# Tiles of an attention and feed-forward kernel moved to multiples of 128 bytes in SBUF

## Chip, cores and metric

One core of a Trainium2 chip. The metric is the device time of one execution in microseconds (us), as a median of several runs. TensorE's granted clock is given by the profile as a share of 2.4 GHz.

## What is computed

Attention over 4 batches, 8 heads, 768 positions and 64 columns a head, with a window of 96 local and 8 global keys and a bias by distance, then a feed-forward layer 512 - 2048 - 512 with ELU, all in float32:

```python
scores = scale * np.matmul(q, k.transpose(0, 1, 3, 2))
bias = -slopes[:, None, None] * dist[None, :, :]
scores = np.where(keep, scores + bias[None, :, :, :], -1000000000.0)
a = np.exp(scores - np.max(scores, axis=-1, keepdims=True))
a = a / (np.sum(a, axis=-1, keepdims=True) + 1e-09)
x = np.matmul(a, v)             # (B, H, S, D) -> (B * S, H * D)
h = x @ w_in
g = np.where(h > 0.0, h, np.exp(np.minimum(h, 0.0)) - 1.0)
out = g @ w_out
```

## The kernel before

The 3072 rows are worked in 12 groups of 256 (two tiles of 128 positions each). For each group the attention of four pairs of heads is computed, and its result is kept in a tile `xh` as a high part (float32r, the type that TensorE takes in one pass) and a low part. The feed-forward layer then runs over 16 chunks of 128 hidden columns: three matmuls make one product in full precision (high x high, low x high, high x low).

There are two stages. In the first (groups 0 to 2, up to about 200 us) the weights are loaded and split into high and low parts on VectorE and ScalarE, and the plain products run: up at L780 (`three`, h<-xh,w), down at L738 (o<-w,gh, 512 columns). In the second (groups 3 to 11) the chunks are taken in pairs, and the down product is a scheme with seven block products in place of eight. Up is again L780 (h<-xh,w0s): the stationary operand is a block of 128 columns of the up weights, which come back from DRAM into a ring of four slots as `w0s`, the moving one is 256 columns of `xh`. Down is L840 (a<-w,gg, a<-ta,gg, a<-tb,gg): here the activations `gg` are stationary and 256 columns of the prepared down weights move. A group has 192 matmuls of L780 and 168 of L840; L780 runs 48 in a row for a pair of chunk pairs (24 in group 11), L840 runs 21 in a row for a chunk pair. Between the two, `z` is worked on by ScalarE (L708, L709) and VectorE (L710), and the attention of a later group is slipped in: its scores (L542; in the first stage L666, in plain float32), transposes (L562, L683) and the products with the values (L585, L700). A few matmuls at L1010 and L1019 fill gaps at the beginning; their results aren't used.

The order on every engine is found in advance by a planner (`Plan.order`) from due times and costs, and then written out as it is. A tile takes one of the named slots of its class (`SLOTS`); a slot is a tag in one of two pools, `w` for the weights (tags that begin with w) and `m` for the rest, laid behind the constants of pool `c`. Tiles are made by `sb` (L306) through `make` when their first writer is written out. `xh` has three slots: in the second stage the odd groups (3, 5, 7, 9, 11) lie in xh0 and the even ones (4, 6, 8, 10) in xh1. A tile begins at a multiple of 32 bytes within a partition, behind the tile before it.

Of the kernel before, what the change touches and what calls it, by code (L numbers as in the profile page):

```python
# [16 lines left out]
P = 128  # L17
# [3 lines left out]
WN = A0 + P  # L21
# [238 lines left out]
def act(n, psum=False, extra=0.0):  # L260
    return (("ACT", (55 if psum else 97) + 0.834 * n + extra, False),)
# [14 lines left out]
class Kernel:  # L276
# [29 lines left out]

    def sb(self, cls, name, shape, dtype=F32, slots=None):
        nm = self.n(name)
        return self.plan.tile(cls, nm, lambda s: (self.w if s[0] == "w" else self.m).tile(shape, dtype, tag=s, name=nm), slots)

    def bank(self, cls, name, shape, slots=None):
        nm = self.n(name)
# [20 lines left out]

    def consts(self):
        self.ident = self.const("ident", [P, P])
        self.tab0, self.tab1 = self.const("tab0", [P, P]), self.const("tab1", [P, WN])

        self.scale = self.const("scale", [P, self.NP])
        self.nmax = self.const("nmax", [P, self.B * self.H * self.S // P])
# [274 lines left out]
    def softmax(self, b, h, t, st_, s, pr, st, i, d):  # L614

        nc, p = self.nc, self.plan
        lo = 0 if t else A0
        n = WN - lo
        at = (b * self.H + h) * (self.S // P) + t
        nm = self.nmax.t[:, at:at + 1]  # L620
        tab = self.tab1.t if t else self.tab0.t
        p.add((("DVE", 158 + 1.042 * n, False),), lambda e: nc.vector.tensor_tensor_reduce(  # L622
            pr.t[:, lo:], st_()[:, lo:], tab, -(2.0 ** -(h + 1)), 3.0e38, ALU.add, ALU.min, nm), [s], [pr], d - 4500)
        p.add(act(n, extra=200), lambda e: nc.scalar.activation(  # L624
            pr.t[:, lo:], pr.t[:, lo:], AF.Exp, bias=nm, scale=-1.0, accum_out=st.t[:, 0, i:i + 1]), [pr], [pr, st], d - 4000)
# [241 lines left out]
    def build(self):  # L867
# [24 lines left out]
        for n, (b, gi) in enumerate(groups):  # L892
# [6 lines left out]
            for hp in range(self.NP):  # L899
# [5 lines left out]
                if n > self.GS:  # L905
                    ahead = start[self.GS] + self.PERIOD * (4 * (n - self.GS - 1) + hp - 2) + self.VISIT
                    d, st = ahead + self.AFTER, 600.0
                todo.append((d if X_.get("rows") else last + 1, lambda b=b, gi=gi, hp=hp, n=n, d=d, st=st, X_=X_, ahead=ahead: self.pair(
                    b, gi, hp, *X[n], d, ahead, st, X_)))
                last = d  # L910
        todo.append((last + 1, lambda: self.visit(lambda: None, 0.0, [], [], last - self.AFTER + self.PERIOD)))
        for fc, d in wdue.items():
# [30 lines left out]

    PERIOD, SECOND, DOWN, DOWN2, VISIT, VALUES = 13200.0, 2890.0, 6730.0, 9250.0, 9245.0, 6720.0
    AFTER = 2 * PERIOD - VISIT + VALUES
    PASSES, SINCE = 2, 195000.0
    GS, KEEP, COMBO = 3, 100000.0, 0.0
    LATE, ASKED = 11, (2, 3, 4)
# [293 lines left out]
```

## Time and profile before

| | us |
|---|---|
| median of three runs | 678.94 (678.84 to 679.95) |
| the profiled execution, whole | 678.11 |
| its span in the trace | 676.3 |
| TensorE busy (share of the span) | 660.5 (98%) |
| weight loads, beside the matmuls | 611.2 (90%) |
| VectorE busy | 516.9 (76%) |
| ScalarE busy | 476.7 (70%) |

Matmuls are pipelined: one of 256 columns is shown with some 280 ns from its start to its end, but the next one starts some 115 ns later. So the time of a run of matmuls is read from the run, not from one of them.

### The profile page before, as it was taken

What the parts mean: (1) busy time and instruction counts of PE and PEld (TensorE: products, weight loads), DVE (VectorE), ACT (ScalarE), POOL (GpSimd) and SP (SyncE); (2) the same over time, 40 slices, a digit from 0 to 9 for tenths busy, and PEclk for the clock granted to TensorE, in tenths of its full rate; (3) what the DMA queues carried; (4) which work ended last, traced back from release to release, by engine and by line L of the source; (5) the groups of instructions that cost most, each with busy time, mean ns of one, the idle gap of its engine ahead of it and who ended that gap; (6) DMA issues with size and microseconds to landing.
All of it is one profiled execution on the core that took longest, in us unless ns stands there. A gap on an engine that the chain in (4) does not pass through costs nothing.

```text
span 676.3 us, 15974 instructions
## 1 busy us (share of the span) xinstructions
PE 660.5 (98%) x5950; PEld 611.2 (90%) x5950; DVE 516.9 (76%) x1515; ACT 476.7 (70%) x1254; POOL 39.4 (6%) x65
## 2 busy tenths in 40 slices
PE   8999999999999999999999999999999999999995
PEld 6677888888888999999999999999999999999995
DVE  7999999999997677667767866866776777765653
ACT  7998888757786667766767766676777767664542
POOL 3143002011210000000000000000000000000000
PEclk9999999999999999999999999999999999999998
DMA  7837978510257665766676657656766765663841
GB/s 265 311 95 259 377 280 322 214 43 19 57 162 244 218 226 170 235 207 228 202 223 232 204 194 223 251 161 211 251 209 203 242 224 163 212 232 135 253 153 37
DMA packets 52233, 137.75 MB, mean 204 GB/s; under 512 B 5682, under 2 KB 18738, under 8 KB 52146
## 3 DMA queue, kind: packets, MB, share of 16 engines
q1 hardware_dynamic: 51856, 136.24, 59.7%
q8 instruction: 49, 0.80, 0.5%
q10 hardware_dynamic: 290, 0.39, 0.2%
q14 instruction: 38, 0.31, 0.1%
HBM read 119.84 MB, written 16.78 MB: 202 GB/s over the span
## 4 chain that ended last, share of the span: by engine, by line
PE 81%; DVE 11%; ACT 3%; DMA 2%; issue 1%; POOL 0%; DVEq 0%; POOLq 0%; SPq 0%
PE h L780 34%; PE a L840 28%; PE o L738 5%; PE pv L585 4%; PE s L542 3%; PE t L562 3%; DVE g L450 2%; DMA rqv<-in_qkv_dram 2%; PE s L666 2%; PE pv L700 1%; DVE gl L331 1%; PE t L683 1%; DVE e L710 1%; ACT pr L624 1%; DVE g L426 1%
## 5 line engine op out<-in xcount | busy, mean ns | idle before, releaser
L780 PE MATMUL h<-xh,w0s 128*128 128x256 f32 x1728 | 210.9, 282 | 0.0
L780 PEld LDWEIGHTS h<-xh,w0s 128*128 128x128 f32 x1728 | 207.3, 190 | 0.1
L840 PE MATMUL a<-w,gg 128*128 128x256 f32 x864 | 140.9, 278 | 0.0
L323 ACT CAST gg<-z 128x384 fp32r<-128x384 f32 (+1 forms) x144 | 81.4, 566 | 73.3 <-PE a L840 35.3
L710 DVE SCALAR_TENSOR_TENSOR z<-z,h 128x512 f32<-128x512 f32 x72 | 49.5, 688 | 106.3 <-ACT z L709 101.9
L840 PEld LDWEIGHTS a<-w,gg 128*128 128x128 f32 x864 | 119.5, 188 | 0.0
L624 ACT ACTIVATE pr<-pr,nmax 128x232 f32<-128x232 f32 (+1 forms) x192 | 90.7, 473 | 6.3 <-DVE nmax L622 6.2
L780 PEld LDWEIGHTS h<-xh,w 128*128 128x128 f32 x576 | 81.6, 189 | 8.8 <-issue 1.4
L331 DVE TENSOR_TENSOR gg<-z,gg 128x512 fp32r<-128x512 f32 (+1 forms) x144 | 84.5, 619 | 5.4 <-ACT gg L323 5.1
L780 PE MATMUL h<-xh,w 128*128 128x256 f32 x576 | 87.4, 284 | 0.1
L708 ACT ACTIVATE z<-h 128x512 f32<-128x512 f32 x72 | 43.0, 597 | 49.0 <-PE h L780 48.3
L811 DVE TENSOR_TENSOR z<-z 128x128 f32<-128x128 f32 (+1 forms) x216 | 72.3, 335 | 5.4
L622 DVE CUSTOM_DVE_ANT_0 pr<-s,tab 128x232 f32<-128x232 f32 (+1 forms) x192 | 62.8, 376 | 15.0 <-PE s L542 14.7
L840 PE MATMUL a<-ta,gg 128*128 128x256 f32 x432 | 72.1, 278 | 0.0
L738 PE MATMUL o<-w,gh 128*128 128x512 f32 x192 | 59.4, 402 | 1.6 <-DVE ob L765 1.2
L840 PEld LDWEIGHTS a<-ta,gg 128*128 128x128 f32 x432 | 59.7, 188 | 0.0
L840 PE MATMUL a<-tb,gg 128*128 128x256 f32 x216 | 53.5, 309 | 0.0
L709 ACT ACTIVATE z<-z 128x512 f32<-128x512 f32 x72 | 45.4, 631 | 2.1
L840 PEld LDWEIGHTS a<-tb,gg 128*128 128x128 f32 x216 | 34.5, 188 | 8.9 <-issue 5.3
L738 PEld LDWEIGHTS o<-w,gh 128*128 128x128 f32 x192 | 32.1, 189 | 6.6 <-ACT pr L624 1.6
L624 ACT ACTIVATION_READ_ACCUMULATOR pr<-pr,nmax 128x1 f32 x192 | 37.1, 193 | 0.0
L608 ACT ACTIVATE pr<-pr,st 128x232 f32<-128x232 f32 (+1 forms) x66 | 29.3, 468 | 10.4 <-DVE st L644 9.1
(122 smaller groups left out, 932.3 us busy)
## 6 DMA issues: line engine op xcount, KB each, us to landing
w0s<-kept SPq DMA_DIRECT2D x144, 512.0 KB, 5.1
rk<-in_qkv_dram SPq DMA_DIRECT2D x45, 184.0 KB, 2.5
bits<-in_w_in_dram SPq DMA_DIRECT2D x16, 512.0 KB, 7.3
bits<-in_w_out_dram SPq DMA_DIRECT2D x16, 512.0 KB, 9.5
kept<-w SPq DMA_DIRECT2D x16, 512.0 KB, 4.3
rv<-in_qkv_dram SPq DMA_DIRECT2D x32, 256.0 KB, 5.0
rqv<-in_qkv_dram SPq DMA_DIRECT2D x13, 384.0 KB, 3.7
rqv<-in_qkv_dram SPq DMA_DIRECT2D x34, 128.0 KB, 3.0
```

The costliest lines, as they stand in the source:

```text
L323: self.nc.scalar.copy(out, x)
L331: self.on(e).tensor_tensor(out, x, y, ALU.subtract)
L608: self.nc.scalar.activation(out, x, AF.Copy, scale=sc)
L622: p.add((("DVE", 158 + 1.042 * n, False),), lambda e: nc.vector.tensor_tensor_reduce(pr.t[:, lo:], st_()[:, lo:], tab, -(2.0 ** -(h + 1)), ...
L624: p.add(act(n, extra=200), lambda e: nc.scalar.activation(pr.t[:, lo:], pr.t[:, lo:], AF.Exp, bias=nm, scale=-1.0, accum_out=st.t[:, 0, i: ...
L708: p.add(act(n, True), lambda e: nc.scalar.activation(out(), hx(), AF.Relu, scale=-1.0), [h], [ex], due)
L709: p.add(act(n), lambda e: nc.scalar.activation(out(), out(), AF.Exp, scale=-1.0), [ex], [ex], due)
L710: p.add(dve(n), lambda e: nc.vector.scalar_tensor_tensor(out(), out(), -1.0, hx(), ALU.add, ALU.max), [h, ex], [ex], due)
L738: nc.tensor.matmul(acc[i].t, g.t[:, i * P:(i + 1) * P], w2.t[:, s], start=fc == f0 and n == 0 and s == HI, stop=fc == f1 - 1 and n == 1)
L780: self.nc.tensor.matmul(hx(), w1.t[:, s, cc * P:(cc + 1) * P], xh.t[:, x, cc], start=n == 0 and cc == 0, stop=n == 2 and cc == self.NCC - 1)
L811: tt = lambda e, out, x, y, op: self.on(e).tensor_tensor(out, x, y, op)
L840: nc.tensor.matmul(acc[i].t[:, j], gg.t[:, x, g], w(s), start=c == x == s == 0 and n in (0, 2, 4, 6), stop=c == N7 - 1 and x == LO and n i ...
```

## The change

The constant `tab1` gets 8 more columns (32 bytes), of which the softmax reads what it read before. `sb` rounds the size of each tile up to a multiple of 128 bytes (`LINE` is 32 elements of four bytes) and gives the kernel the view of the shape that it asked for. A list of names, `ODD`, that would begin 64 bytes later is empty. Instructions, their order on each engine, their waits and the slots are the same as before; the addresses in SBUF differ. Where the built programs place the tiles, as bytes past a multiple of 128:

| tile | before | after |
|---|---|---|
| all slots of the weights (w0, w1, w0s, ta, tb, bits) | 96 | 0 |
| xh0, xh1, xh2 | 96, 32, 96 | 0 |
| gg; gh and gl | 32 | 0 |
| z in its slots z0, vd0, xh2 | 96, 32, 96 | 0 |
| qs, ks, rv, part | 32 | 0 |
| rqv, rk of the first stage | 96 (two of them 32) | 0 |
| pr in the second stage | 32 and 64 | 0 |
| tab0, tab1, ident | 0 | 0 |

`pr` grows from 928 to 1024 bytes, `rk` from 1472 to 1536, `st` from 48 to 128; the rest were multiples of 128 already, and change by where they begin.

```diff
     def sb(self, cls, name, shape, dtype=F32, slots=None):
         nm = self.n(name)
-        return self.plan.tile(cls, nm, lambda s: (self.w if s[0] == "w" else self.m).tile(shape, dtype, tag=s, name=nm), slots)
+        n = 1
+        for x in shape[1:]:
+            n *= x
+        first = self.LINE // 2 if name in self.ODD else 0
+
+        def make(s):
+            t = (self.w if s[0] == "w" else self.m).tile([P, -(-(first + n) // self.LINE) * self.LINE], dtype, tag=s, name=nm)[:, first:first + n]
+            if len(shape) > 2:
+                names = "abcd"[:len(shape) - 1]
+                t = t.rearrange(f"p ({' '.join(names)}) -> p {' '.join(names)}", **dict(zip(names, shape[1:])))
+            return t
+
+        return self.plan.tile(cls, nm, make, slots)
...
-        self.tab0, self.tab1 = self.const("tab0", [P, P]), self.const("tab1", [P, WN])
+        self.tab0, self.tab1 = self.const("tab0", [P, P]), self.const("tab1", [P, WN + self.LINE // 4])
...
-        tab = self.tab1.t if t else self.tab0.t
+        tab = self.tab1.t[:, :WN] if t else self.tab0.t
...
     AFTER = 2 * PERIOD - VISIT + VALUES
+    LINE, ODD = 32, ()
```

## Rows read from the trace of the kernel before

**Rows 1.** The page: span, busy time and share of TensorE, its clock in 40 slices.

```profile
span 676.3 us, 15974 instructions
...
PE 660.5 (98%) x5950; PEld 611.2 (90%) x5950; DVE 516.9 (76%) x1515; ACT 476.7 (70%) x1254; POOL 39.4 (6%) x65
...
PEclk9999999999999999999999999999999999999998
```

**Rows 2.** Stretches from:to us: length, busy us (and instructions) per engine, clock, DMA.

```profile
75.00:200.00 125.00, 123.45 (x850) 107.38 (x851) 124.00 (x316) 94.68 (x256) 14.57 (x18) 1.00 0.48 175
200.00:660.00 460.00, 458.90 (x4499) 440.60 (x4498) 317.70 (x936) 313.44 (x793) 1.62 (x3) 1.00 0.64 210
```

**Rows 3.** The page's chain of work that ended last, by engine and by line.

```profile
PE 81%; DVE 11%; ACT 3%; DMA 2%; issue 1%; POOL 0%; DVEq 0%; POOLq 0%; SPq 0%
PE h L780 34%; PE a L840 28%; PE o L738 5%; PE pv L585 4%; PE s L542 3%; PE t L562 3%; DVE g L450 2%; DMA rqv<-in_qkv_dram 2%; PE s L666 2%; PE pv L700 1%; DVE gl L331 1%; PE t L683 1%; DVE e L710 1%; ACT pr L624 1%; DVE g L426 1%
```

**Rows 4.** That chain in order of time: start us, length us, engine, tile, line, count.

```profile
494.32 5.45 PE h L780 x48
...
519.79 5.75 PE h L780 x48
533.14 5.75 PE h L780 x48
...
539.92 2.67 PE a L840 x21
543.90 2.58 PE a L840 x21
...
586.43 5.65 PE h L780 x48
...
632.05 2.88 PE h L780 x24
```

**Rows 5.** Timeline of TensorE: start us, length us, then what; even and odd group.

```profile
481.44 5.61 PE L780 MATMUL h<-xh,w0s 128*128 128x256 f32 x48
...
531.28 0.62 PE L840 MATMUL a<-ta,gg 128*128 128x256 f32 x4
...
532.98 5.92 PE L780 MATMUL h<-xh,w0s 128*128 128x256 f32 x48
...
540.66 0.63 PE L840 MATMUL a<-ta,gg 128*128 128x256 f32 x4
```

**Rows 6.** Timeline of weight loads at the filler matmuls; line L1019, mean of one below.

```profile
31.26 1.30 PEld L1019 LDWEIGHTS o<-w 128*128 128x128 f32 x11 [0.17 <-issue]
...
L1019 PEld LDWEIGHTS o<-w x11: 187/192/193, 31.3 to 32.4; 128*128 128x128 f32 x11
```

**Rows 7.** Chain up to 215 us: shares by line, then pieces in order of time.

```profile
by line: PE o L738 15.5%; PE h L780 15.2%; DVE g L450 6.4%; DMA rqv<-in_qkv_dram 5.2%; PE s L666 5.0%; PE pv L700 4.0%; DVE gl L331 3.8%; issue 3.5%; PE t L683 3.4%; DVE e L710 3.2%; ACT pr L624 2.9%; DVE g L426 2.5%; DVE w L331 2.3%; DVE g
...
12.28 4.15 DMA rqv<-in_qkv_dram
...
19.06 3.35 DMA rqv<-in_qkv_dram
...
34.69 0.98 PE s L666 x8
36.49 0.94 PE h L780 x8
...
38.45 0.98 PE s L666 x8
40.10 1.39 PE o L738 x6
```

**Rows 8.** Line views of L710 and L709 on z: ns min/median/max, first and last start.

```profile
L709 ACT ACTIVATE z<-z x72: 620/632/635, 206.1 to 662.2; 128x512 f32<-128x512 f32 x72
L710 DVE SCALAR_TENSOR_TENSOR z<-z,h x72: 670/689/690, 206.7 to 662.9; 128x512 f32<-128x512 f32 x72
```

**Rows 9.** DMA issues: count, size, median us to landing.

```profile
w0s<-kept SPq DMA_DIRECT2D x144, 512.0 KB, 5.1
```

## Prediction

> **What bounds the kernel now.** I read the page's first two parts, then the busy times by stretch, then the chain of work that ended last, first by line and then in order of time. TensorE is busy 660.5 of 676.3 us at a granted clock of 1.00, that is 2.4 GHz, and only the last slice shows less [rows 1]. From 200 to 660 us it stands still for about 1 us of 460, while VectorE is busy 317.7 and ScalarE 313.4 us; from 75 to 200 us VectorE is as full as TensorE, 124.0 of 125 us [rows 2]. The chain says the same: 81% TensorE, and two lines hold 62% of the span, the up products of L780 (34%) and the down products of L840 (28%) [rows 3]. So in the long second stage the spacing of these matmuls is the time. There are 1728 of L780 and 1512 of L840 in it, all 128x128 weights against 256 columns.
>
> The rows that matter are those of the same work at different speeds. In order of time, a run of 48 matmuls of L780 takes 5.75, 5.65 or 5.45 us, and a run of 21 of L840 takes 2.67 or 2.58 us [rows 4]. Per matmul 5.75 is 119.8 ns, 5.65 is 117.7, 5.45 is 113.5. The timeline gives the same with the pipeline's end in it: 5.92 against 5.61 us for 48, 0.63 against 0.62 for 4 of L840 [rows 5]. The clock is full in all of them and nothing is waited for, so only the operands differ. Instruction, shape and weight slots are the same in all groups of query blocks; what alternates is the slot of xh, the moving operand. Odd groups (3, 5, 7, 9, 11) read xh0, which starts 96 bytes past a multiple of 128, the offset of the weights; even groups (4, 6, 8, 10) read xh1, at 32. Each of the 17 runs of 48 and 6 of 24 on xh0 is of the slow kind (16 of them are in the list of long pieces). Of the 16 on xh1, 11 are 5.65 and 5 are 5.45. L840 has its moving weights at 96 and its stationary gg at 32, also different, and never the slow kind: counted from the starts of its matmuls, 40 of 72 runs are at 117.7 ns, 32 at 113.4.
>
> **What I take from that.** The start addresses of the two operands that TensorE reads at the same time (the columns of this matmul and the weights of the next) set the spacing. At 2.4 GHz 113.4 ns is 272 columns and 119.9 ns is 288: 17 and 18 times 16 columns of four bytes, so a step of 64 bytes. My reading, an estimate from these rows, is that operands are fetched in aligned pieces of 64 or 128 bytes, that 1024 bytes beginning 32 bytes off need a piece more, and that two streams that cross their borders together collide for another. Starting on a border takes the extra piece away.
>
> The Trainium skill, "SBUF — State Buffer", section "Who interferes with whom", says otherwise: TensorE never waits on anyone, and its two read ports are independent. By that the change is worth nothing and the sum is 678.1. The 5.75 and 5.45 us of equal work disagree [rows 4].
>
> **The change, part by part.**
> L780 on xh0: all operands now at 0. If each run goes at the fast spacing that the trace has, 17 x (5.75 - 5.45) + 6 x (2.88 - 2.72) = 5.1 + 0.9 = 6.0 us. L780 on xh1: 11 x (5.65 - 5.45) = 2.2 us. L840: 40 x (2.67 - 2.58) = 3.6 us. Together 11.8 us, all on the path: TensorE has no idle time there that it could fall into, VectorE and ScalarE have a third of the stretch free, and the weights of the ring land 5.1 us after their issue while a period of two chunks is 13.3 us (the distance of two 5.75 rows) [rows 2, 4, 9]. What is late next is still TensorE.
>
> How fast an aligned pair is, no row shows. From below, the weight load bounds it: the eleven filler matmuls of L1019 stream only 128 columns and their weight loads still come (1.30 - 0.19) / 10 = 111 ns apart [rows 6]. At 111 ns the gain is 17 x 0.42 + 6 x 0.22 + 11 x 0.32 + 5 x 0.12 + 21 x (40 x 0.0067 + 32 x 0.0024) = 8.5 + 4.1 + 7.2 = 19.8 us. From above it is 119.8 ns for all (the rival below). I take 113.4, a spacing that is there already and needs only that the worse two go. The Trainium skill, "TensorE: Matmul & The Clock Gate", section "Back-to-back issue gap", gives 262 cycles for 256 columns, which is 109 ns, and would make it some 26 us; the weight load of 111 ns speaks against so much.
>
> The first 200 us: in the chain up to 215 us L780 and L738 have 15.2 and 15.5% [rows 7], 32.7 and 33.3 us, of which 5.8 us belong to the first run of the second stage. So some 226 matmuls at about 118 ns (0.94 for 8) and 144 with 512 columns at 232 (1.39 for 6) [rows 7]. At 4.6 ns less each that is 1.0 + 0.7 = 1.7 us, but VectorE is full there and takes over; I count half, 0.8 us. The bounds are 0 and 3.5 (226 x 4.6 ns and 144 x (232 - 213), where 213 ns is 512 columns at 2.4 GHz).
>
> The other matmuls (L542, L562, L585, L666, L683, L700): half arrays or plain float32, some of them on operands at 0 or 64 already. L666 takes 0.98 us for 8 wherever it stands, though its keys begin at 96 in one half of the eight and at 0 in the other [rows 7]; I put these at 0, within 0.5 us either way. VectorE and ScalarE: z lies at 96 in one slot and at 32 in another, and 72 instructions of L710 take 670 to 690 ns, of L709 620 to 635 [rows 8]. They don't see these offsets; 0. DMA: the queues' bytes and order stay. On the chain they stand in three pieces of 3.4 to 4.2 us at the start [rows 7]; a tenth of that either way is 1 us, I take 0. Tiles grow by at most 96 bytes, and no slot, wait or instruction moves.
>
> **Sum:** 678.11 us of the profiled execution - 11.8 - 0.8 = 665.5. That execution is 0.83 us under the median of the three (678.94), so I expect a median of about 666.3 us, 1.9% less.
>
> **The rivals.**
> Equal offsets collide, on a border or off it. The slow kind is the one where both operands have the same offset, and now all have. For it: without exception, 17 runs of 48 and 6 of 24. Against: the fillers of L1019 read both operands from one tile at 96 and are 111 ns apart, so that equal offsets alone don't cost 7 ns; and the extra piece that gives two streams an uneven first step is gone. It decides if the pair at 0 and 0 behaves as the pair at 96 and 96: then L780 on xh1 loses 11 x 0.10 + 5 x 0.30 = 2.6 us and L840 21 x (40 x 2.1 + 32 x 6.4) ns = 6.1 us, while xh0 gains nothing: 8.7 us, 687.6 us.
> The middle spacing stays. The same operands of L840 run now at 113.4 and now at 117.7 for a whole run, which looks like two ways in which the streams can fall into step, and aligned ones may have both. With all at 117.7 xh0 gains 17 x 0.10 + 6 x 0.05 = 2.0, xh1 loses 1.0 and L840 32 x 0.09 = 2.9: 1.9 us slower, 680.8. With half of the runs so, about 5 us gained, 674.
> Nothing happens. If xh0 and xh1 differ for another reason than their offset to 128 (the slot's place in the memory, what writes nearby), or by the page's rule above, padding changes nothing: 678.9. Against it speaks that L840, in its own slots, keeps to the two faster kinds.
>
> **How the numbers follow.** Forecast 0.56, the middle spacing 0.16, equal offsets collide 0.20, nothing 0.08. The range goes from 678.9 - 19.8 - 3.5 = 655.6 (weight load as the bound, all of the early gain) to 681.0 (all at the middle spacing) and leaves out the collision. A measurement of this kernel tells about 0.2% (1.4 us) from no change. Faster: 0.56 + 0.13 of the middle spacing = 0.69. Same: 0.06 of nothing and 0.03 of the middle = 0.09. Slower: 0.20 + 0.02 = 0.22.
>
> **What would show it.** In the chain of the changed kernel, the runs of 48 should be 5.45 us or a little less in odd and even groups alike, and those of 21 2.58 or less. Rows of 5.75 everywhere, L840 at 2.7 and above, mean the collision; a mix of 5.65 and 5.45 the middle. If odd groups are still slower than even ones, the offset to 128 was not the reason. The forecast is wrong, too, if matmuls get faster and the span doesn't: then VectorE's waits for ScalarE's z or TensorE's idle time must have grown.

## The result: 1.1% slower, and what the profile after shows

| | before | after |
|---|---|---|
| median, us (4 runs each) | 678.89 (677.8 to 679.95) | 686.5 (684.7 to 687.12) |
| ratio, 95% interval | | 1.0111 (1.0096 to 1.0125) |
| the profiled execution, its span | 678.11, 676.3 | 684.7, 682.9 |
| TensorE busy, us | 660.5 | 668.0 |

The forecast of 666.3 us was wrong in size and in sign: the range went to 681.0, and the time lies above it. What came true is the rival "equal offsets collide", priced at 687.6.

The page of the kernel after answers [rows 1] and [rows 3] (line numbers are now 12 higher: L780 is L792, L840 is L852, L738 is L750).

```profile
span 682.9 us, 15974 instructions
...
PE 668.0 (98%) x5950; PEld 618.5 (91%) x5950; DVE 517.0 (76%) x1515; ACT 476.8 (70%) x1254; POOL 39.0 (6%) x65
...
PEclk9999999999999999999999999999999999999999
...
PE 83%; DVE 11%; ACT 2%; DMA 2%; issue 1%; POOL 0%; DVEq 0%; POOLq 0%; SPq 0%
```

The same 5950 matmuls at the same clock are busy for 7.5 us more; VectorE and ScalarE differ by 0.1 us. So the loss lies in the matmuls themselves, and not in a wait or in another engine. The stretches, which answer [rows 2], say where:

```profile
75.00:200.00 125.00, 123.49 (x850) 107.40 (x849) 123.92 (x316) 94.51 (x256) 14.38 (x18) 1.00 0.49 175
200.00:660.00 460.00, 458.92 (x4441) 440.42 (x4440) 313.78 (x926) 310.30 (x788) 1.81 (x3) 1.00 0.64 209
```

The first stage is as it was (850 matmuls in 75 to 200 us, 850 before). In the 460 us after it TensorE is as busy as before and gets 58 matmuls less done, 4441 against 4499. The chain in order of time (start us, length us, engine, tile, line, count) shows which:

```profile
504.89 2.70 PE a L852 x21
...
508.80 2.69 PE a L852 x21
511.50 5.76 PE h L792 x48
...
524.79 5.70 PE h L792 x48
...
531.51 2.71 PE a L852 x21
```

```profile
655.11 2.85 PE h L792 x24
657.96 2.51 PE a L852 x21
...
668.69 6.49 PE a L852 x54
675.18 0.04 DVEq L869
```

Even groups (xh1) now take 5.76 us for 48 where [rows 4] has 5.45 or 5.65. Odd groups (xh0) take 5.70 where it has 5.75, and 2.85 for 24 where it has 2.88. The runs of 21 of L852 are at 2.69 to 2.71 where they were 2.67 or 2.58 (2.51 in the last group, 2.38 before). The mixture is gone: all 16 runs on xh1 stand at 5.76, 16 of 17 on xh0 at 5.70; the other one, the first of the stage, at 5.78.

The sum of the rows is the result. xh1: 16 x 5.76 less (11 x 5.65 + 5 x 5.45), +2.8 us. xh0: 16 x 0.05 + 6 x 0.03, about -1.0. L852, counted from the starts of its matmuls, goes from 115.8 to 119.7 ns: 1512 x 3.9 ns, +5.9. Together +7.7. The last matmuls of the kernel before show the same distance:

```profile
661.54 6.13 PE a L840 x54
667.68 0.04 DVEq L857
```

The last run ends at 667.68 before and 675.18 after, 7.5 us later. The span grew by 6.6 only because what follows (the last sums and the output's transfer) took 7.7 us in the profiled execution after and 8.6 in the one before; the medians differ by 7.6.

### The profile page after: what moved, and what is told of

It is laid out like the page before. It is cut to its first block, busy times and chain, and to the rows that moved or that the text cites. A ratio compares the mean times of both kernels' runs of the same rounds, so it can differ in the third digit from the quotient of the medians.

```text
span 682.9 us, 15974 instructions
## 1 busy us (share of the span) xinstructions
PE 668.0 (98%) x5950; PEld 618.5 (91%) x5950; DVE 517.0 (76%) x1515; ACT 476.8 (70%) x1254; POOL 39.0 (6%) x65
## 4 chain that ended last, share of the span: by engine, by line
PE 83%; DVE 11%; ACT 2%; DMA 2%; issue 1%; POOL 0%; DVEq 0%; POOLq 0%; SPq 0%
PE h L792 35%; PE a L852 28%; PE o L750 5%; PE pv L597 4%; PE s L554 3%; PE t L574 3%; DVE g L462 2%; DMA rqv<-in_qkv_dram 2%; PE pv L712 1%; DVE gl L343 1%; PE t L695 1%; ACT pr L636 1%; DVE e L722 1%; PE s L678 1%; DVE g L438 1%
## 5 line engine op out<-in xcount | busy, mean ns | idle before, releaser
L792 PE MATMUL h<-xh,w0s 128*128 128x256 f32 x1728 | 212.5, 282 | 0.0
L792 PEld LDWEIGHTS h<-xh,w0s 128*128 128x128 f32 x1728 | 209.0, 190 | 0.1
L852 PE MATMUL a<-w,gg 128*128 128x256 f32 x864 | 144.7, 283 | 0.0
L722 DVE SCALAR_TENSOR_TENSOR z<-z,h 128x512 f32<-128x512 f32 x72 | 49.5, 688 | 111.6 <-ACT z L721 110.7
L852 PEld LDWEIGHTS a<-w,gg 128*128 128x128 f32 x864 | 122.8, 191 | 0.0
L792 PEld LDWEIGHTS h<-xh,w 128*128 128x128 f32 x576 | 81.7, 189 | 8.8 <-issue 1.4
L792 PE MATMUL h<-xh,w 128*128 128x256 f32 x576 | 87.6, 284 | 0.0
L852 PE MATMUL a<-ta,gg 128*128 128x256 f32 x432 | 73.9, 283 | 0.0
L852 PEld LDWEIGHTS a<-ta,gg 128*128 128x128 f32 x432 | 61.5, 192 | 0.0
L750 PE MATMUL o<-w,gh 128*128 128x512 f32 x192 | 59.5, 402 | 1.6 <-DVE ob L777 1.1
L852 PE MATMUL a<-tb,gg 128*128 128x256 f32 x216 | 54.1, 312 | 0.0
L852 PEld LDWEIGHTS a<-tb,gg 128*128 128x128 f32 x216 | 34.7, 189 | 8.9 <-issue 5.3
L750 PEld LDWEIGHTS o<-w,gh 128*128 128x128 f32 x192 | 32.2, 189 | 6.8 <-ACT pr L636 1.5
L335 ACT COPY pt<-t 116x512 f32<-116x512 f32 (+2 forms) x80 | 34.8, 442 | 2.4 <-PE t L695 0.9
```

The costliest lines, as they stand in the source:

```text
L335: self.nc.scalar.copy(out, x)
L722: p.add(dve(n), lambda e: nc.vector.scalar_tensor_tensor(out(), out(), -1.0, hx(), ALU.add, ALU.max), [h, ex], [ex], due)
L750: nc.tensor.matmul(acc[i].t, g.t[:, i * P:(i + 1) * P], w2.t[:, s], start=fc == f0 and n == 0 and s == HI, stop=fc == f1 - 1 and n == 1)
L792: self.nc.tensor.matmul(hx(), w1.t[:, s, cc * P:(cc + 1) * P], xh.t[:, x, cc], start=n == 0 and cc == 0, stop=n == 2 and cc == self.NCC - 1)
L852: nc.tensor.matmul(acc[i].t[:, j], gg.t[:, x, g], w(s), start=c == x == s == 0 and n in (0, 2, 4, 6), stop=c == N7 - 1 and x == LO and n i ...
```

## The experiments

All have the instructions and the order of the kernel after; only addresses (and with them the sizes of padded tiles) differ, save in the sweep. In what follows **the difference** is where the moving operand of a matmul begins less where the stationary block of the next one begins, in bytes modulo 256. I first looked at starts modulo 128, as the prediction did. The built programs give these differences:

| | L792 on xh0 | L792 on xh1 | L852 |
|---|---|---|---|
| before (as L780, L840) | 0 | 192 | 64 |
| after | 128 | 0 | 0 |

**Both activations half a line later.** xh and gg begin 64 bytes behind the border, all else on it. The difference becomes 64 for L792, and 64 or 192 for L852, by the slot of gg. Both tiles get another 128 bytes of padding by it.

```diff
-    LINE, ODD = 32, ()
+    LINE, ODD = 32, ("xh", "gg")
```

> The changed kernel, with xh and gg beginning 64 bytes past a multiple of 128 and all else at 0. So in L792 the moving operand is 64 bytes off the stationary one, and in L852 the other way round, as xh1 and gg were to the weights before, but with every operand on a multiple of 64. Theory A (the difference of the two start addresses to 128 sets the spacing, wherever they lie): no run of 48 at 5.70 or 5.76 us is left, all are between 5.45 and 5.65, those of 21 between 2.58 and 2.67; 667 to 675 us, faster than both kernels. Theory B (a start on a multiple of 64 is itself slow, the collision has nothing to do with the difference): runs stay at 5.7 and the time at 685 to 688.

677.21 us, ratio 0.9982 (0.9967 to 0.9997): the whole loss is gone, though every tile still begins on a multiple of 64 and the padding is larger. Its chain:

```profile
506.24 5.65 PE h L792 x48
...
512.70 2.60 PE a L852 x21
...
516.61 2.67 PE a L852 x21
```

31 of 32 long runs of 48 on the list are at 5.65. L852 alternates between 2.60 and 2.67 with the slot of gg: 114.3 ns at the difference 192, 117.5 at 64. So the padding isn't the cause. What is left is the border of 128 bytes itself or the relative position, and the next run separates these.

**Everything 32 bytes off the border.** `tab1` gets 16 more columns instead of 8, and all tiles behind it begin 32 bytes past a multiple of 128. All differences are those of the kernel after.

```diff
-self.const("tab1", [P, WN + self.LINE // 4])
+self.const("tab1", [P, WN + self.LINE // 2])
```

> The changed kernel, with the constant tab1 another 32 bytes longer, so that every tile begins at 32 past a multiple of 128 in place of 0: the differences are as in the changed kernel, the borders are missed. Theory A: nothing changes, 685 to 688 us, runs of 48 at 5.70 to 5.76. Theory B (a start on the border is what is slow): back to the spacing of the kernel before or better, 5.45 to 5.65, 670 to 680 us.

685.94 us, ratio 1.0111 (1.0094 to 1.0128), the same as after. Its chain:

```profile
512.96 5.76 PE h L792 x48
...
523.54 2.71 PE a L852 x21
526.25 5.70 PE h L792 x48
```

The rows are those of after to 0.02 us. Whether a tile begins on the border is worth nothing here, neither gain nor loss. That a start on the border takes an extra piece away, on which the forecast stood, is refuted for this shift. With the run before it: relative position is the cause.

**Only xh half a line later.** gg stays on the border.

```diff
-    LINE, ODD = 32, ()
+    LINE, ODD = 32, ("xh",)
```

> As the first, with xh alone at 64 and gg at 0. Theory A: the runs of 48 (L792) get 5.45 to 5.65 as in the first, those of 21 (L852) stay at 2.65 to 2.72; 677 to 683 us. If L852 gets faster too, then it is the slots' place in the memory and not the difference.

680.7 us, ratio 1.0027 (1.0014 to 1.004). Its chain:

```profile
508.89 5.65 PE h L792 x48
...
519.37 2.72 PE a L852 x21
522.08 5.44 PE h L792 x48
...
528.55 2.69 PE a L852 x21
```

The line whose operand was moved recovers (21 runs of 48 at 5.65, 11 at 5.44 or 5.45), the other stays slow. A larger xh pushed gg along by 128 bytes, so that L852 stands at the difference 128 and not 0; 2.68 to 2.72 us a run, on average 118.9 ns a matmul, is little better than the 119.7 of the difference 0. Each line pays for its own pair of operands. From here I took the difference modulo 256, since 128 and 0 differ on L792 as well (5.70 and 5.76).

**Scans of the difference.** Each slot of xh and gg gets an offset of its own, in elements of four bytes. The edit is the same in all of the following, with other numbers; here the first scan.

```diff
-        first = self.LINE // 2 if name in self.ODD else 0
...
         def make(s):
+            first = self.OFF.get(s, 0) if name in ("xh", "gg") else 0
...
-    LINE, ODD = 32, ()
+    LINE, OFF = 32, {"xh0": 8, "xh1": 24, "gg0": 8, "gg1": 24}
```

> The changed kernel with the slots at four differences: xh0 at 32, xh1 at 96, gg0 at 32 and gg1 at 96 past a multiple of 128, weights at 0. It asks how the spacing depends on the difference. Theory A in its sharpest form (two halves of 64 bytes; a start inside the same half collides): xh0 and gg0 (same half) as slow as at 0, 5.7 us; xh1 and gg1 (other half) 5.45 to 5.65. If the distance counts and not the half, all four lie alike, between 5.45 and 5.76. 672 to 684 us.

681.22 us, ratio 1.0046 (1.002 to 1.0071). The differences are 160 and 224 for L792, 224 and 32 for L852, and the spacings 117.8, 118.4, 118.2 and 117.3 ns: between the slow and the fast ones, and none falls into 113.4. So there are no two halves of 64 bytes of which one is slow and one fast.

The second scan moves by 48, 80, 16 and 112 bytes, to multiples of 16 that aren't multiples of 32.

```diff
+    LINE, OFF = 32, {"xh0": 12, "xh1": 20, "gg0": 4, "gg1": 28}
```

> Four more differences between the moving and the stationary operand, to 128 bytes: 48 on xh0, 80 on xh1, 112 for gg0 and 16 for gg1. If the spacing falls evenly as the difference goes from 0 to 64, 48 and 80 are near 116 ns and 16 and 112 near 119. If only a start within the same 16 bytes collides, all four are at 113 to 118. 674 to 683 us.

683.14 us, ratio 1.008 (1.0058 to 1.0102): 119.2 and 119.1 ns for L792 (runs of 48 at 5.71 to 5.73), 118.2 and 118.3 for L852. Neither expectation fits, the even fall or the free pass outside 16 bytes, and nothing is gained by these four.

**192 everywhere and 64 everywhere.** The two differences that gave L852 its two spacings in the run with both at 64, now one at a time and for both lines. (In the last group part of gg lies in a third slot: 60 of the 1512 matmuls of L852 have the other difference.)

```diff
+    LINE, OFF = 32, {"xh0": 16, "xh1": 16, "gg0": 16, "gg1": 48}
```

> All tiles on multiples of 128 but the slots of xh and gg, which are placed so that in the whole second stage the moving operand begins 192 bytes behind the stationary one, to 256 (64 short of it). In the run with both at 64 the part of L852 that had 192 took 114.3 ns a matmul on average, and the part that had 64 took 117.5. If the difference to 256 decides (theory C): all runs near 5.45 and 2.58 us, 666 to 670 us, faster than the kernel before. If it is chance which of the two spacings a run falls into, 5.45 and 5.65 mixed, 671 to 677 us.

```diff
+    LINE, OFF = 32, {"xh0": 48, "xh1": 16, "gg0": 16, "gg1": 48}
```

> The counterpart: 64 bytes behind to 256, in both L792 and L852. Theory C: nearly all runs at 5.65 and 2.67 us, 677 to 679 us. Chance: mixed as in the one with 192, 671 to 677 us.

192: 673.36 us, ratio 0.9936 (0.9912 to 0.9959), faster than both kernels. 64: 678.51 us, ratio 1.0008 (0.9996 to 1.0019). The chain at 192, then the chain at 64:

```profile
504.29 5.46 PE h L792 x48
510.55 2.59 PE a L852 x21
...
530.24 5.65 PE h L792 x48
536.92 2.60 PE a L852 x21
```

```profile
504.18 2.58 PE a L852 x21
...
510.56 5.44 PE h L792 x48
516.81 2.67 PE a L852 x21
...
523.47 5.65 PE h L792 x48
```

The sign of the difference matters for L852: 114.3 ns at 192, 117.4 at 64. L792 doesn't follow. Of the 32 runs of 48 on the list it has 5.65 in 30 and 5.44 to 5.46 in two, at either difference. So theory C holds for L852 and fails for L792, and 5.65 isn't a matter of the address alone: the same operands run at both.

**A sweep in one place.** Before the first down product 1080 matmuls are added, whose results nobody uses: one stationary block throughout, the moving operand from the same tile, its start moved from 0 to 512 bytes, 20 matmuls at each start; then other widths at 0 and 64 bytes; then the whole list backwards.

```diff
+        todo = [
+            lambda: mm(out[:, :256], st, f[:, 0:256], start=True, stop=True),
+            lambda: mm(out[:, :256], st, f[:, 4:260], start=True, stop=True),
...
+            lambda: mm(out[:, :512], st, f[:, 16:528], start=True, stop=True),
+        ]
+        for one in todo + todo[::-1]:
+            for _ in range(20):
+                one()
```

> The changed kernel with a block of measuring matmuls put in ahead of the first down product: one fixed stationary block of the first up weights, and a moving operand from the same tile whose start is moved on by 0, 16, 32 ... 512 bytes (256 columns), then 128, 192, 224, 384 and 512 columns at 0 and 64 bytes; 20 of each in a row, the whole list forwards and then backwards. Their products are overwritten, and nothing of the computation is changed; the time is some 130 us longer. Theory A: 20 at 0 take 2.40 us (120.0 ns each), at 64, 192, 320 and 448 bytes 2.27 or 2.35 (113.4 or 117.7), whatever came before them; at 128 and 384 near 2.37 (118.7), at 256 and 512 as at 0. With fewer columns than 224 the difference goes away (111 ns, the weight load). If instead each row depends on the block before it, forwards and backwards differ.

828.16 us in its one run. The timeline of TensorE (start us, length us with the pipeline's end in it). The starts are 0 bytes (L1042), 64 (L1046), 112 (L1049), 192 (L1052), 448 (L1057), 512 (L1058), then 128 columns at 0 and 64 (L1059, L1060) and 512 columns at 0 (L1067):

```profile
33.75 2.60 PE L1042 MATMUL o<-w 128*128 128x256 f32 x20
...
43.26 2.52 PE L1046 MATMUL o<-w 128*128 128x256 f32 x20
...
50.38 2.48 PE L1049 MATMUL o<-w 128*128 128x256 f32 x20
...
57.41 2.46 PE L1052 MATMUL o<-w 128*128 128x256 f32 x20
...
69.19 2.46 PE L1057 MATMUL o<-w 128*128 128x256 f32 x20
71.48 2.54 PE L1058 MATMUL o<-w 128*128 128x256 f32 x20
73.87 2.35 PE L1059 MATMUL o<-w 128*128 128x128 f32 x20
76.05 2.40 PE L1060 MATMUL o<-w 128*128 128x128 f32 x20
...
94.23 4.71 PE L1067 MATMUL o<-w 128*128 128x512 f32 x20
...
147.01 2.52 PE L1052 MATMUL o<-w 128*128 128x256 f32 x20
...
154.09 2.46 PE L1049 MATMUL o<-w 128*128 128x256 f32 x20
...
170.64 2.56 PE L1042 MATMUL o<-w 128*128 128x256 f32 x20
```

One of these matmuls takes some 280 ns, so (2.56 - 0.28) / 19 = 120.0 ns is the spacing at 0 bytes on the way back, and (2.46 - 0.28) / 19 = 114.7 that at 112. Counted from the starts of the single matmuls, without the first distance of each block, the means are, on the way there and back:

| start moved by, bytes | ns, there / back |
|---|---|
| 0, 256, 512 | 119.3, 119.3, 119.0 / 120, 119.2, 118.9 |
| 64, 320 | 117.9, 117.8 / 117.8, 117.8 |
| 112 | 116.1 / 114.8 |
| 128, 384 | 118.3, 118.3 / 118.8, 118.6 |
| 192, 448 | 114.8, 114.8 / 117.8, 114.0 |
| 16, 32, 48, 80, 96, 160, 224 | 116.7 to 120.0 |
| 0 and 64, with 128 to 224 columns | 111.6 to 112.0 |
| 0, with 384 columns; 64, with 384 | 174.9 / 174.8; 173.3 / 173.2 |
| 0 and 64, with 512 columns | 227.2, 229.1 / 227.8, 229.1 |

Three things follow. The spacing repeats every 256 bytes. At 112, 192 and 448 a block begins slower and after 4 to 10 matmuls drops to 113.4 and stays, save 192 on the way back; at 0 it settles at 120. And 192 settles at 113.4 on the way there and at 117.7 on the way back, with the same two operands: there are two steady ways to run. With 224 columns or fewer neither 0 nor 64 matters, and with 384 both settle at 173.3 ns. My reading, which no run proves: 111.7 ns is the weight load's own spacing, half of the 512-column spacing is 113.6, so at 256 columns the two streams are about equally long, and there their meeting costs something.

In the sweep other engines have no part in it. The two blocks at 192 (from:to us: length, then busy us and instructions of TensorE, its weight loads, VectorE, ScalarE and GpSimd, clock, DMA) ran while nothing else did:

```profile
57.40:59.70 2.30, 2.30 (x22) 2.30 (x21) 0.00 (x0) 0.00 (x0) 0.00 (x0) 1.00 0.00 0
147.00:149.30 2.30, 2.30 (x22) 2.30 (x21) 0.00 (x0) 0.00 (x0) 0.00 (x0) 1.00 0.00 0
```

So the slow spacing and the two ways need no one but TensorE. What differs between these two blocks is what TensorE ran before them (a start at 160 bytes there, at 224 on the way back). That this decides is likely, but argued from one pair of blocks.

**Taking the best of it.** L792 at 112, L852 at 192; and both at 112.

```diff
+    LINE, OFF = 32, {"xh0": 60, "xh1": 28, "gg0": 48, "gg1": 48}
```

> Theory (the difference of the two starts, modulo 256, sets the spacing; 112 is one that falls into the fast spacing by itself, as the sweep's two blocks at 112 did after 10 and 6 matmuls): L792 at 112, L852 at 192 as in the run with 192 everywhere. Runs of 48 of L792 then take 5.45 to 5.5 us in place of 5.65, L852 stays at 114.3 ns: 673.4 - 1728 x (117.3 - 114) ns = 667.7 us. Rival (what a run of matmuls enters from decides, the difference only which two spacings are open): L792 follows L852 and settles at 117.7 again, runs of 48 stay at 5.65, 673 us. Second rival (112 isn't a multiple of 32 and what the sweep showed is chance, as with 16 and 48 in the run of small steps): 5.7 us a run, 676 us.

```diff
+    LINE, OFF = 32, {"xh0": 60, "xh1": 28, "gg0": 4, "gg1": 36}
```

> Theory (112 is a fast difference for either line): L792 and L852 both at 112, runs of 48 at 5.45 to 5.5 us and runs of 21 at 2.58: about 667 us, like the run with 112 and 192. Rival (entry decides): L852 at 112 or L792 at 112 settles in the middle, 117.7 ns, in part or throughout: 670 to 679 us. If L792 is fast here and wasn't with 192 on L852, the pair of neighbours decides; if L852 is slower here than at 192, 192 is its own difference.

112 and 192: 671.2 us, ratio 0.9901 (0.9879 to 0.9924), the fastest of all. Its chain:

```profile
508.28 2.59 PE a L852 x21
...
514.79 5.49 PE h L792 x48
521.30 2.60 PE a L852 x21
```

Both at 112: 676.77 us, ratio 0.9986 (0.9973 to 0.9999). Its chain:

```profile
505.09 5.50 PE h L792 x48
511.39 2.68 PE a L852 x21
...
524.58 2.71 PE a L852 x21
```

L792 is fast at 112 in every run of 48 (5.47 to 5.51, 114.6 ns), whichever spacing L852 has beside it. That excludes, at this difference, the rival by which a run takes over its neighbour's spacing. The time was expected at 667.7 us, 5.7 under the run at 192; by the medians it is 2.2 under it, by the spans 2.8 (672.2 and 669.4). Between the first run of 48 in its chain and the last run of 54 the second stage did become 4.3 us shorter; the step of L792 was from 117.3 to 114.6 ns and not to 114, and what lies before and behind that stretch took 1.5 us more in this execution. L852 at 112 has 119.4 ns, so 112 is no fast difference for it. In that run its stationary gg begins 16 bytes past a multiple of 32, while the stationary blocks of L792 and of the sweep begin at multiples of 32; whether that is the reason wasn't tried.

## Why the prediction was wrong

**What bounds the kernel** was right. The change came out of the spacing of two lines in the second stage, and, to 0.2 us, of nothing else.

**That the two start addresses set the spacing** was right too. But what counts is their difference and not, as the prediction had it, where they lie to a border. The run with 64 bytes (0.9982) and the run with everything 32 off (1.0111) show it together: still on multiples of 64, other differences, other time; other alignment, same differences, same time. Offsets were taken to 128 bytes, and the period is 256. That is why xh0 went from 5.75 to 5.70 and no further than that: it came from 0 to 128, from one slow difference to another.

**The step that failed** is the estimate behind it: that operands are fetched in aligned pieces and that a start on a border takes the extra piece away. It was read from 272 and 288 columns being 17 and 18 times 64 bytes, two numbers that fitted, with no row of an aligned pair. It turned the evidence around. All rows showed that equal starts are slow, without exception (23 runs on xh0), and the change makes all starts equal; the estimate alone let that be worth a gain. In its place the runs showed that equal starts are as slow on the border as off it: 5.76 us for 48 at the difference 0, with both operands at 0 and with both at 32, as 5.75 with both at 96 before. So xh1 and L840, which had been at 192 and 64, lost 2.8 and 5.9 us.

**The argument against the collision** failed with it. The fillers of L1019 read both operands from one tile and are 111 ns apart [rows 6]; from that the prediction took that equal starts don't cost 7 ns. After the change their weight loads have the same length beside 5.76 us of L792 (timeline of the weight loads after):

```profile
31.42 1.30 PEld L1032 LDWEIGHTS o<-w 128*128 128x128 f32 x11 [0.17 <-issue]
```

The sweep says why: with 128 columns the spacing is 111.6 to 112.0 ns at 0 as at 64 bytes. A row with another width said nothing about 256 columns. The same row also bounded the gain from below, and that use stands: no line of 256 columns settled under 113.3 ns.

**The terms.** L780 on xh0: -6.0 expected, about -1.0 measured. On xh1: -2.2 expected, +2.8 measured. L840: -3.6 expected, +5.9 measured. The rival's own working had 0, +2.6 and +6.1, so its two large terms were right to 0.2 us. The first 200 us: -0.8 expected, none seen (850 matmuls in 75 to 200 us in both). The upper bound of that term was also added up wrongly: 226 x 4.6 ns and 144 x 19 ns make 3.8 and not 3.5 us, so the range's lower end should have been 655.3. It changes nothing here. VectorE and ScalarE at 0 was right (L710 took 670 to 690 ns [rows 8]; now the line view of L722 has):

```profile
L722 DVE SCALAR_TENSOR_TENSOR z<-z,h x72: 669/689/690, 206.9 to 670.0; 128x512 f32<-128x512 f32 x72
```

The Trainium skill's rule ("SBUF — State Buffer", "Who interferes with whom"), by which TensorE waits on no one and its read ports are independent, would have made the change worth nothing. The traces disagree again: 5.49 us (L792 at 112) and 5.76 us (at 0) for 48 equal matmuls, by the distance of their operands alone.

**The middle spacing** was seen as a rival and is real: two steady ways to run the same operands, 113.4 and 117.7 ns. It didn't decide here, since at the differences 0 and 128 neither occurs.

**What stays open**: why 256 bytes, what makes a run fall into the one way or the other at 192 and 64, and why 112 serves L792 and not L852. L852 takes the fast way at 192 in 62 of some 70 runs, L792 in 2 of 32. L792 at 64 takes it in 1 of 32 long runs when L852 stands at 64 and 192, and in 11 of 32 when L852 stands at 128: the difference of its own operands alone doesn't decide that.

## What to carry to other kernels

Where equal instructions run at several speeds in one trace and only their operands differ, tabulate the speed against each operand's address and against their difference before thinking of a mechanism. If every slow row shares a property, expect a change that gives this property to all rows to be slower, until a row shows otherwise. A row that is to speak against this must have the same shape: here the width that was 128 and not 256 columns hid the effect.

## What was not expected of the hardware

- For matmuls of 256 columns with a new stationary block each, the distance between the start of the moving operand and the start of the next block moves the spacing, with a period of 256 bytes: about 120 ns at 0, 118.8 at 128, mostly 117.7 at 64, on average 114.3 to 114.6 at its best (192 for L852, 112 for L792). From 120 to 113.4 is 6% of the matmul, and by the ratios (1.0111 and 0.9901) some 14 us of this kernel between its slowest and fastest layout. It needs no other engine: in the sweep the 120 ns at 0 and both ways at 192 stand while VectorE, ScalarE, GpSimd and the DMA queues are idle.
- Position itself doesn't show in the one shift tried: 32 bytes for all tiles together changed no run of 21 or 48 by more than 0.02 us, whereas 64 bytes for two of them changed the time by 9 us.
- The same pair of operands can run steadily at 113.4 or at 117.7 ns, and can drop from the slower to the faster in the middle of a run (after 4 to 10 matmuls in the sweep).
- With 128 to 224 columns the spacing is 111.6 to 112.0 ns at both differences tried, 0 and 64; with 512 the order is the other way round and small, 227.2 at 0 and 229.1 at 64.
